# A long convolution: blocked sine-table transforms replaced by one two-stage transform of 4096 points with on-chip shuffles

## The chip, the cores and the metric

One core of one Trainium2 chip. The metric is device time in microseconds (us) from the first to the last instruction plus a fixed start and end (the profiled span is some 1.8 us shorter). Every time of a kernel below is a median of several executions, and every kernel is compared with the kernel before in executions that alternate on the same chip. An execution is called slow when it is over 1.5% above the fastest of the same kernel; ratios use the fast ones.

## The reference

All tensors are bf16, sequence S = 2048, width D = 448, MLP width F = 1792.

```python
def reference(A_q, A_k, A_v, A_shift_k, A_ssm_k, A_ssm_D, B_x, B_w1, B_b1, B_w2, B_b2):
    # mixer on layernorm(q)
    k_shift = sum over t of k_pad[:, t:t+S] * shift_k[:, 3-t]          # 4 taps
    kv   = k_shift * v                                                 # [S, D]
    y    = irfft(rfft(kv padded to 4096) * rfft(ssm_k padded to 4096))[:S]
    y    = y + kv * ssm_D
    h    = A_q + layernorm(A_q) * y
    # MLP along the sequence
    u    = gelu_tanh(einsum("bsd,sf->bdf", layernorm(h), w1) + b1)     # 448 x 1792
    return h + transpose(einsum("bdf,fs->bds", u, w2) + b2)
```

(Shortened: padding, casts and transposes are left out.) The heavy parts are the convolution of 448 channels over 2048 points and the two MLP products.

## The kernel before

The convolution is done in four blocks of 512 points. Each block is transformed by dense products with sine and cosine tables, block spectra are multiplied and summed through the identity matrix on TensorE, and each output tile is transformed back.

```python
def emit_forward(sig, r_sig, blk, dstA, dstB, ...):          # 4 phases x 4 tiles x 2 tables
    for tab, r_tab, dst, r_d in ((NC_t, ..., dstA, ...), (NSf_t, ..., dstB, ...)):
        for phi in range(NPHI):
            for tp in range(TPB):
                op("pe", ... e.matmul(bank(4 + phi), tab[:, tp, 128 * phi: 128 * phi + 128],
                                      sig[:, TPB * blk + tp, :], start=(tp == 0), stop=(tp == TPB - 1)))
            op("act", ... e.copy(out=dst[:, phi, :], in_=bank(4 + phi)))

def emit_products_b(b):                                       # (cut) for every pair of blocks c, j = b - c:
    ...                                                       # 4 products on VectorE, summed on TensorE:
    op("pe", ... e.matmul(bank(bre), ident,  mset[:, 0, q, :], start=first, stop=False))
    op("pe", ... e.matmul(bank(bre), nident, mset[:, 1, q, :], start=False, stop=last))
    ...

def emit_inverse_T(T):                                        # 8 or 16 matmuls per output tile
    ...
def emit_gelu(q, fc):                                         # six instructions, ScalarE and VectorE by turns
    ...
```

w1 is streamed in 32 pieces of 224 KB through a ring; q (normalised) and h go out to DRAM and come back.

## Time and profile before

| | before |
|---|---|
| time, median of 3 (range) | 297.61 us (297.02 to 297.87) |
| TensorE busy | 229.9 us, 78% of the span, 1154 instructions |
| VectorE, ScalarE busy | 178.4 us, 159.4 us |
| granted TensorE clock, mean of later runs | 0.95 to 0.96 |
| DMA | 39.36 MB |
| matmuls of 448 columns | 1088 |

The prediction below shows the lines and reads them.

### The profile page before, as it was taken

Reading aid. Unit: us, or ns where it says so; the run is one execution under the profiler, and the core shown is the slowest. Engines: PE = TensorE matmul, PEld = TensorE weight load, DVE = VectorE, ACT = ScalarE, POOL = GpSimd, SP = SyncE. Lnnn points to the kernel's source line nnn. Section 1 sums busy time; section 2 is a strip of 40 time slices with the busy share of each in tenths; the row PEclk is TensorE's granted clock in tenths of the full one; section 3 lists DMA queues with packets and bytes.
Section 4 is the critical chain, followed back from the end, with each engine's and each line's share of the span. In section 5 each row is a group of like instructions: output and inputs, shape, how many; then the busy total and the mean of one; then the engine's idle time right before and its main releaser. Section 6 shows DMA issues by size and latency. Waiting matters only on the chain.

```text
span 295.9 us, 3832 instructions
## 1 busy us (share of the span) xinstructions
PE 229.9 (78%) x1154; PEld 112.8 (38%) x1154; DVE 178.4 (60%) x426; ACT 159.4 (54%) x335; POOL 33.1 (11%) x81
## 2 busy tenths in 40 slices
PE   0024169999779999899928969759929999799995
PEld 0023124455325555445503425325514444345552
DVE  8959986685998974987187772442244124454131
ACT  2389266998753585867682683854656135610000
POOL 6001120000000032221223031321100000000000
PEclk9999999999979999999975989979987999999999
DMA  6721776658043333221220199436984420025322
GB/s 183 193 74 71 224 232 190 199 173 265 7 149 94 111 113 91 78 78 32 65 62 1 47 320 363 113 109 194 328 329 127 141 107 2 0 62 147 105 62 78
DMA packets 28552, 39.36 MB, mean 133 GB/s; under 512 B 3060, under 2 KB 23670, under 8 KB 28532
## 3 DMA queue, kind: packets, MB, share of 16 engines
q1 hardware_dynamic: 22100, 24.44, 27.5%
q10 hardware_dynamic: 6432, 14.68, 14.7%
q8 instruction: 9, 0.15, 0.2%
q14 instruction: 11, 0.09, 0.1%
HBM read 33.61 MB, written 5.51 MB: 132 GB/s over the span
## 4 chain that ended last, share of the span: by engine, by line
PE 44%; DVE 10%; DMA 8%; ACT 5%; issue 2%; POOL 1%; DVEq 1%; SPq 0%; ACTq 0%
PE ps_all L1046 13%; PE ps_all L1063 12%; PE ps_all L945 8%; PE ps_all L834 4%; DMA XB<-in_B_w_dram 4%; DMA qs<-out_dram 3%; PE ps_all L908 2%; PE ps_all L914 2%; PE ps_all L917 2%; PE ps_all L911 2%; DVE XB L888 1%; DVE XB L890 1%; DMA xs<-in_A_q_dram 1%; DVE XB L886 1%; DVE t1s L962 1%
## 5 line engine op out<-in xcount | busy, mean ns | idle before, releaser
L1046 PE MATMUL ps_all<-hn,XB 128*128 128x448 bf16 x224 | 50.3, 379 | 14.1 <-DMA XB<-in_B_w_dram 6.3
L1063 PE MATMUL ps_all<-XB,YB 128*128 128x448 bf16 x224 | 43.6, 353 | 2.5 <-DVE XB L1036 2.5
L1046 PEld LDWEIGHTS ps_all<-hn,XB 128*128 128x128 bf16 x224 | 22.5, 104 | 40.7 <-issue 13.9
L945 PE MATMUL ps_all<-XB,NC_t 128*128 128x448 bf16 x112 | 32.1, 364 | 1.8 <-ACT XB L924 1.1
L945 PE MATMUL ps_all<-XB,NSi_t 128*128 128x448 bf16 x112 | 32.3, 363 | 0.0
L752 PE MATMUL ps_all<-ident,XB 128*128 128x128 bf16 (+1 forms) x64 | 7.0, 293 | 31.7 <-DMA XB<-in_A_ssm_k_dram 17.3
L1063 PEld LDWEIGHTS ps_all<-XB,YB 128*128 128x128 bf16 x224 | 21.4, 98 | 24.3 <-DVE XB L1036 4.6
L834 PE MATMUL ps_all<-kv,NC_t 128*128 128x448 bf16 x64 | 19.9, 366 | 6.9 <-DVE t1s L962 6.9
L1066 DVE SCALAR_TENSOR_TENSOR osb<-ps_all,b2col,hs 128x448 bf16<-128x448 f32 x16 | 10.5, 681 | 21.6 <-PE ps_all L1063 21.6
L924 ACT CAST XB<-ps_all 128x448 bf16<-128x448 f32 x32 | 16.9, 530 | 10.8 <-PE ps_all L911 8.0
L834 PE MATMUL ps_all<-XB,NC_t 128*128 128x448 bf16 x64 | 21.3, 398 | 0.7 <-ACT XB L761 0.7
L840 ACT ACTIVATE YB<-ps_all,sc 128x448 bf16<-128x448 f32 x32 | 18.7, 632 | 4.8 <-PE ps_all L834 4.7
L844 ACT CAST YB<-ps_all 128x448 bf16<-128x448 f32 x32 | 16.6, 534 | 8.4 <-PE ps_all L834 8.3
L834 PE MATMUL ps_all<-kv,NSf_t 128*128 128x448 bf16 x64 | 19.9, 366 | 0.7 <-ACT YB L844 0.7
L790 DVE TENSOR_TENSOR XB<-XB,Wt 128x1792 bf16<-128x1792 bf16 x16 | 17.1, 1079 | 4.9 <-DMA XB<-in_A_k_dram 4.8
L834 PE MATMUL ps_all<-XB,NSf_t 128*128 128x448 bf16 x64 | 19.9, 352 | 0.0
L1029 DVE SCALAR_TENSOR_TENSOR XB<-XB 128x448 bf16<-128x448 bf16 x14 | 8.8, 625 | 15.9 <-ACT XB L1023 8.4
L752 PEld LDWEIGHTS ps_all<-ident,XB 128*128 128x128 bf16 (+1 forms) x64 | 5.7, 139 | 32.8 <-DMA XB<-in_A_ssm_k_dram 18.4
L821 ACT ACTIVATE qs<-xs,nm_x,rs_x 128x448 bf16<-128x448 bf16 x16 | 12.1, 760 | 9.3 <-DVE nm_x L818 9.0
L908 PE MATMUL ps_all<-XB,ident 128*128 128x448 bf16 x40 | 14.5, 364 | 3.1 <-DVE XB L896 2.8
L945 PEld LDWEIGHTS ps_all<-XB,NC_t 128*128 128x128 bf16 x112 | 11.2, 100 | 13.9 <-ACT XB L924 1.5
L970 ACT ACTIVATE junk<-hs 128x448 bf16<-128x448 bf16 x16 | 9.2, 575 | 12.5 <-DVE hs L966 5.6
(103 smaller groups left out, 386.3 us busy)
## 6 DMA issues: line engine op xcount, KB each, us to landing
XB<-in_B_w_dram ACTq DMA_DIRECT2D x32, 224.0 KB, 2.9
YB<-in_B_w_dram ACTq DMA_DIRECT2D x2, 3584.0 KB, 13.6
XB<-in_A_k_dram SPq DMA_DIRECT2D x15, 448.0 KB, 4.0
xs<-in_A_q_dram SPq DMA_DIRECT2D x32, 112.0 KB, 2.2
XB<-in_A_v_dram SPq DMA_DIRECT2D x16, 112.0 KB, 3.2
out_dram<-qs SPq DMA_DIRECT2D x16, 112.0 KB, 1.7
qs<-out_dram SPq DMA_DIRECT2D x16, 112.0 KB, 2.4
out_dram<-hs SPq DMA_DIRECT2D x16, 112.0 KB, 1.9
```

What stands on the lines that cost most here:

```text
L752: op("pe", lambda e, dst=dst, slot=slot, tt=tt, w=w: e.transpose(out=dst, in_=knat[0:w, slot, 128 * tt: 128 * tt + 128], identity=ident[0: ...
L790: op(E, lambda e: e.tensor_tensor(out=prod, in0=ktap[:, slot, :, :], in1=Wt, op=ALU.mult), reads=[r_ktap[slot], r_Wt], writes=[r_prod[ei]] ...
L821: op("act", lambda e: e.activation(out=qs[:, slot, :], in_=xs[:, slot, :], func=ACT.Identity, bias=nm_x[:, t:t + 1], scale=rs_x[:, t:t + 1 ...
L834: op("pe", lambda e, bk=bk, lhsT=lhsT, tile=tile, tp=tp: e.matmul(bank(bk), lhsT, sig[:, tile, :], start=(tp == 0), stop=(tp == TPB - 1)), ...
L840: op("act", lambda e, bk=bk, dst_ap=dst_ap, scl=scl: e.activation(out=dst_ap, in_=bank(bk), func=ACT.Copy, scale=scl), reads=[Rbank[bk], r ...
L844: op("act", lambda e, bk=bk, dst_ap=dst_ap: e.copy(out=dst_ap, in_=bank(bk)), reads=[Rbank[bk]], writes=[r_d], n=D)
L908: op("pe", lambda e, bre=bre, mset=mset, q=q, first=first: e.matmul(bank(bre), ident, mset[:, 0, q, :], start=first, stop=False), reads=[r ...
L924: op("act", lambda e, bk=bk, dst=dst: e.copy(out=dst, in_=bank(bk)), reads=[Rbank[bk]], writes=[r_Pst[pslot]], n=D)
L945: op("pe", lambda e, lhsT=lhsT, rhs=rhs, ti=ti: e.matmul(bank(bk), lhsT, rhs, start=(ti == 0), stop=(ti == n - 1)), reads=[r_l, r_r], writ ...
L1046: op("pe", lambda e, q=q, slot=slot, t=t: e.matmul(bank(q), w1s[:, slot, 128 * q: 128 * q + 128], hn[:, t, :], start=(t == 0), stop=(t == ...
L1063: op("pe", lambda e, fc=fc: e.matmul(bank(bk), w2sb[:, fc, 128 * T: 128 * T + 128], gT[:, fc, :], start=(fc == 0), stop=(fc == NFC - 1)), ...
L1066: op("dve", lambda e: e.scalar_tensor_tensor(out=osb[:, ob, :], in0=bank(bk), scalar=b2col[:, T:T + 1], in1=hs2[:, fs, :], op0=ALU.add, op ...
```

## The change

Intent: fewer matmuls. With 4096 = 16 x 256 the transform becomes two cheap stages with a shuffle between them: row p of a 16-row group goes from partition to free dimension. The shuffle is a DMA copy from SBUF to SBUF. Everything stays on chip, w1 and w2 are fetched whole, gelu is one ScalarE instruction, and a new list scheduler orders all engines and hands out PSUM banks and staging buffers as it goes. (PSUM is the memory into which TensorE writes its results; the kernel deals it out as eight banks. An eviction is the copy of a result from PSUM to SBUF, by ScalarE or VectorE.) The diff, cut to its core:

```diff
-def emit_forward(...)   # dense 512-point blocks: 256 matmuls
-def emit_products_b(b)  # sums over block pairs through the identity: 160 matmuls
-def emit_inverse_T(T)   # 224 matmuls
+def emit_stage1(src, o_src, T, o_T, tag):
+    for r in range(R):                                   # R = 16
+        b = _Buf(psum, 2)                                # two PSUM banks, given out by the scheduler
+        w = _Buf(wring)                                  # one of 8 staging buffers
+        op("pe", ... e.matmul(Pb(b, 0), Ct[:, r, :], src[:, r, :], start=True, stop=True))
+        op("pe", ... e.matmul(Pb(b, 1), St[:, r, :], src[:, r, :], start=True, stop=True))
+        op(FX, fn, ...)                                  # eviction of 896 elements, ScalarE or VectorE
+        op("sp", ... e.dma_start(T[r:128:R] ..., WR(w.slots[0]) ...), ..., keng=8)   # the shuffle, 229 KB
+def emit_stage2(T, o_T, scale):                          # 16 x 4 matmuls, 16 evictions
+def emit_products_i1():
+    for j in range(R):                                   # 2 products on VectorE, 8 matmuls, 1 eviction
+        ...
+        op("sp", ... e.dma_start(TZ[j:128:R] ..., TU[:, j] ...), ..., keng=8)        # inverse shuffle
+def emit_i2():
+    for g in range(8):
+        for i in range(2):
+            r = 2 * g + i
+            b = _Buf(psum)
+            op("pe", ... e.matmul(Pb(b), ID,  V[:, r, :],         start=True,  stop=False))  # kv * D
+            op("pe", ... e.matmul(Pb(b), CTt[:, r, :], TZ[:, r, 0, :], start=False, stop=False))
+            op("pe", ... e.matmul(Pb(b), STt[:, r, :], TZ[:, r, 1, :], start=False, stop=True))
+            ...                                          # times q, plus x, layernorm
-def emit_gelu(q, fc):    # Identity, Square, 2 x VectorE, Sigmoid, multiply
+def emit_gelu(b, fc):    # one activation
+    op("act", ... e.activation(out=G[:, fc, :], in_=Pb(b), func=ACT.Gelu_apprx_tanh, bias=b1c[:, fc:fc + 1]))
+def emit_w1_load(which) / emit_w2_load():                # whole weights, on ScalarE's DMA queue
+        Pb(b), W2[:, fc, r:S:R], G[:, fc, :], ...        # second product: weight columns 16 apart
+psum = _Pool(8); wring = _Pool(8)
+def can_acquire(o):                                      # an operation may start when its banks are free
+    ...
```

The order in which things are emitted: K's stages, U's first stage (K is the transform of ssm_k, U that of kv), the products with the first inverse step, the second inverse step (`emit_i2`), the MLP.

## The prediction

Passages of the prediction and of the expectations that no trace or run of this case shows are cut, and the places are marked. The sum of the prediction came to 274 us with shuffles of 2.1 us and to 243 with shuffles of 1.43, weighed to 262. Two of its terms are the 2.1 us, and the 0.91 us of an eviction of 896 elements on ScalarE, of which 15 are the 14 us of U's second stage. Both were my assumptions at that point; the trace after shows 2.1 us (229 KB at 108 GB/s from 40 to 60 us) and 0.905 us (L621).

> **What bounds the kernel now.** I read the span in stages first (busy time of each engine in five stretches), because its limits differ by stage, then the chain that ended last, then the groups of instructions for durations.
>
> ```profile
> core 0: us, PE busy (x) PEld busy (x) DVE busy (x) ACT busy (x) POOL busy (x), PEclk, DMA share, GB/s
> 0.00:44.00 44.00, 10.65 (x76) 7.28 (x77) 38.18 (x78) 24.30 (x46) 8.49 (x23) 1.00 0.55 162
> 44.00:196.00 152.00, 131.77 (x646) 63.22 (x643) 106.42 (x278) 103.07 (x233) 22.20 (x53) 0.94 0.40 127
> 196.00:247.00 51.00, 44.52 (x213) 21.16 (x214) 16.17 (x42) 23.85 (x45) 2.36 (x6) 0.90 0.57 187
> 247.00:262.00 15.00, 12.51 (x63) 5.53 (x62) 7.11 (x16) 8.13 (x14) 0.00 (x0) 1.00 0.00 0
> 262.00:296.00 34.00, 30.49 (x162) 15.56 (x159) 10.48 (x16) 0.00 (x0) 0.00 (x0) 0.98 0.33 99
> ```
>
> Up to 44 us VectorE makes sine tables and TensorE idles. From 44 to 196 us the blocked convolution runs: TensorE is busy 131.8 of 152 us with 646 matmuls, so this stage is bound by the count of matmuls. From 196 us on it is the MLP: 100 us for 448 matmuls. The chain shows the dense pace and the holes:
>
> ```profile
> 204.33 10.96 PE ps_all L1046 x58
> 215.29 6.37 DMA XB<-in_B_w_dram
> 221.71 12.12 PE ps_all L1046 x52
> 233.83 4.52 DMA XB<-in_B_w_dram
> ...
> 248.48 0.63 ACT XB L1026
> 249.12 0.47 ACT XB L1034
> 249.61 0.40 DVE XB L1036
> ...
> 261.67 30.83 PE ps_all L1063 x162
> ```
>
> A dense 448-column matmul costs 10.96/58 = 0.189 us, or 30.83/162 = 0.190; in the stretch with the lower clock 12.12/52 = 0.233. Two waits for w1 (6.4 and 4.5 us) and the six-step gelu (14 us between 247 and 262, matmuls in it counted) are MLP overhead. Unit costs for the sum:
>
> ```profile
> L844 ACT CAST YB<-ps_all 128x448 bf16<-128x448 f32 x32 | 16.6, 534 | 8.4 <-PE ps_all L834 8.3
> L790 DVE TENSOR_TENSOR XB<-XB,Wt 128x1792 bf16<-128x1792 bf16 x16 | 17.1, 1079 | 4.9 <-DMA XB<-in_A_k_dram 4.8
> L888 DVE TENSOR_TENSOR XB<-YB 128x896 bf16<-128x896 bf16 x20 | 12.3, 623 | 0.5
> L962 DVE TENSOR_TENSOR t1s<-kv,ps_all 128x448 bf16<-128x448 bf16 x16 | 9.8, 616 | 2.3 <-PE ps_all L945 2.3
> L966 DVE TENSOR_TENSOR hs<-t2s,xs 128x448 bf16<-128x448 bf16 x16 | 6.2, 390 | 2.8 <-DMA xs<-in_A_q_dram 1.4 <-DVE t2s L964 0.5 <-ACT hn L987 0.4
> L970 ACT ACTIVATE junk<-hs 128x448 bf16<-128x448 bf16 x16 | 9.2, 575 | 12.5 <-DVE hs L966 5.6 <-PE ps_all L1046 2.2 <-DVE mv_h L978 2.1
> L970 ACT ACTIVATION_READ_ACCUMULATOR junk<-hs 128x1 f32 x16 | 3.0, 186 | 0.0
> q1 hardware_dynamic: 22100, 24.44, 27.5%
> ```
>
> [...] The second MLP product now reads weights 32 bytes apart; all weights before were packed (about 100 ns), so this is unverified.
>
> **The change part by part.**
>
> *TensorE.* Before: 128+128 matmuls forward, 160 product sums, 224 inverse, 448 MLP = 1088 of 448 columns. After: two signals x (32 + 64) = 192, products with the first inverse step 128, second inverse step 48, MLP 448 = 816, plus 96 transposes. Removed: 272 x 0.19 = 52 us. If TensorE stayed the bound, this alone would give 297 - 52 = 245.
>
> *DMA.* Removed: k read four times (16 x 448 KB becomes 1.8 + 0.3 MB), and q and h through DRAM. Added: 48 shuffles of 128 x 1792 B = 229 KB, 11.0 MB. Sum 8.3 (inputs) + 14.7 (weights) + 1.8 (out) + 11.0 = 36 MB against 39.4: no saving, and the shuffles are now on the path, since each second stage needs all 16 shuffles of the first. Cost of one: queue 1 moved 24.44 MB in 27.5% of 16 x 295.9 us, 18.8 GB/s per engine (queue 10: 21), so eight engines at 20 take 1.43 us[...]. I use 2.1 as the likelier, 1.43 as the rival.
>
> *Path.* Estimates from these costs and from the built order.
> - Loads ahead of the shuffles on SP's queue: 8.3 MB at some 310 GB/s (between the early 209 GB/s at a 0.75 share, 279, and 339 on queue 10): done at 29 us. K's transposes and evictions (4 of 1792 elements) are ready at about 21 us, so the shuffles wait behind the load of x.
> - kv: tables end on VectorE near 11.5 us, then 24 x 1.08 + 16 x 0.62 = 36 us: ready at 47.5. [...]
> - Shuffles of K and U: eight staging slots; evictions from the ninth on wait for a shuffle's semaphore in the built order. 32 x 2.1 = 67 us from 29 on, plus about 6 for w1's first half, issued late in this stretch onto the same engines, plus landing: U complete at about 102 us. TensorE is mostly idle here. VectorE's three evictions of late U slots stand in order ahead of its layernorm work and stall it until 81 us.
> - Second stage of U (64 matmuls, 15 evictions on ScalarE, 14 us), 32 products x 0.623 = 20 us. In VectorE's order a block of layernorm and kv*D work (about 13 us: 9 statistics of 0.6, 5 x 0.62, small ones) stands between the fourth and fifth product. Last product near 137 us.
> - Inverse shuffles: start at 120, ten x 2.1, +4 for w1's second half, landing: 146. ScalarE's queue then holds a w2 load that waits for those ten, ahead of the evictions of the last five; these five then share the engines with 4.2 MB of weights, about 3 us each: everything landed at 165.
> - Second inverse step: VectorE does 15 x (0.616 + 0.39) = 15 us before its first normalisation, so the MLP starts near 165 + 18.5 = 184; ScalarE's statistics, 32 x 0.76 = 24 us, last until 192 and are covered by the first 96+ matmuls.
> - MLP: 448 x 0.194 = 87 us. All w1 and w2 are in time; gelu is one 0.6 us instruction and its matmuls are interleaved, so the holes (11 us of DMA, about 14 of gelu) go. Last addition and store 3 us. Sum: 184 + 87 + 3 = 274.
>
> With 1.43 us per shuffle, U is complete near 82, the last inverse shuffle at 134, the MLP starts at 153: 243.
>
> **The rivals.** *Shuffles are engine-limited or spread over 16 engines*: 243 or less; for it, queue rates of about 20 GB/s per engine and a program that allows for eight engines[...]. *TensorE remains the bound*: 245, by the arithmetic above; against it, the three points where a whole stage must land before the next can start. *Strided weights slow the second MLP product*: if a load rose from 0.1 to 0.4 us, 224 x (0.4 - 0.19) = 47 us would be added, 290 to 320. For it, nothing before has such weights; against it, [...]loads overlap matmuls (PEld busy 15.6 of 34 us at the end)[...]. *Weights beside the last inverse shuffles*: without this contention the first sum would be about 262.
>
> **Range and chances.** I weigh 274 at 0.6 and 243 at 0.4: 262 us. The range 238 to 285 covers both with some error in the load rate (3 us) and clock (0.85 instead of 1 in half of the MLP: +8). 285 leaves out most of the strided-weight case, to which I give 8%. Below 291.7 is faster by over 2%: 0.89; within 2%: 0.06; slower: 0.05.
>
> **What would show each step.** TensorE about 170 us busy for 912 instructions; a hole in its activity before U's second stage (near 75 to 100 us) and another before the second inverse step; in both, the chain naming the on-chip copy (arena from arena). Time from issue to landing of the shuffles of 2 us when alone and far more when queued; 16 in a row spaced 2.1 us[...] or 1.4 us (engines). DMA share near 0.5 in this stretch if only eight engines work. MLP matmuls at 0.19 us and weight loads of the last product still about 0.1 us. No gelu hole. The prediction is wrong below 238 if shuffles are cheaper than 1.4 us or run on 16 engines, and above 285 if weight loads or landing times are longer than assumed.

## More of the kernel before

TensorE has 44% of the span on the chain of work that ended last, DMA 8%. One line adds to this, the clock granted to TensorE in 40 slices of the span, in tenths (9 is 90% or more):

```profile
PEclk9999999999979999999975989979987999999999
```

TensorE, busy for 78% of the span, was granted 0.95 of its full clock over it.

## The result, and the profile after

The changed kernel is correct and slower: **321.1 us** (317.69 to 326.04, 5 executions) against 297.61 (296.29 to 298.53, 5 executions of the same session). The ratio of the fast runs is 1.0749, 95% interval 1.0682 to 1.0816. A ratio is the mean time of one kernel's fast runs over that of the other's of the same rounds, so it is not quite the ratio of the medians. The recorded trace is one of two executions of 326 us that count as slow (granted clock 0.783 against 0.80 in the fast ones), so its stage times are up to some 2% long; the effects below are far larger.

| | predicted | measured after |
|---|---|---|
| one shuffle | 2.1 us (rival 1.43) | 2.1 us |
| U complete (last shuffle of U landed) | 102 | 104.8 |
| first inverse shuffle issued | 120 | 150.9 |
| last inverse shuffle landed | 165 | 213.7 |
| MLP on the chain from | 184 | 229.3 |
| MLP to the end | 90 | 95 |
| TensorE busy | about 170 us | 213.5 us (x913) |
| time | 262 (274 with 2.1 us shuffles) | 321.1 |

The page of the changed kernel, two rows of the slices and the chain that ended last by engine and line (DMA as a whole has 31% of it, 8% before):

```profile
PEclk9978555559795665555599959559599999999999
DMA  7996555555996000001229579629500000000022
...
DMA arena<-arena 28%; PE ps L1034 13%; ACT arena L621 10%; PE ps L888 10%; PE ps L854 8%; PE ps L1025 8%; PE ps L1017 6%; DMA arena<-in_A_ssm_k_dram 3%; ACT arena L839 3%; DVE arena L958 2%; DVE arena L961 1%; PE ps L817 1%; DVE arena L1037 1%; SPq L743 0%; DVE arena L624 0%
```

"arena<-arena" is the shuffle: 28% of the span. The DMA row has six slices at 5, further on five at 0, and then rises again: two shuffle phases with a gap between them in which no data moves. The clock row shows 5 or 6 in the gap.

Two stretches, busy time of each engine, granted clock, DMA share and rate:

```profile
core 0: us, PE busy (x) PEld busy (x) DVE busy (x) ACT busy (x) POOL busy (x), PEclk, DMA share, GB/s
40.00:60.00 20.00, 8.29 (x19) 1.19 (x18) 7.04 (x9) 8.15 (x9) 0.00 (x0) 0.50 0.54 108
120.00:140.00 20.00, 12.98 (x32) 3.50 (x32) 7.65 (x24) 6.33 (x7) 4.40 (x7) 0.50 0.00 0
```

From 40 to 60 us the shuffles of K and U run alone: 108 GB/s, at a share of 0.54, near the 0.5 that was foreseen for eight engines of sixteen (no view here shows the engines singly). 229 KB at 108 to 110 GB/s is 2.1 us each, the likelier figure of the prediction. From 120 to 140 us nothing moves by DMA and no engine is near full: TensorE 65%, at half its clock, ScalarE 32%, VectorE 38%. This is the stretch to explain. The chain there:

```profile
119.09 0.91 ACT arena L621
...
120.05 1.69 PE ps L854 x4
121.76 0.91 ACT arena L621
...
150.94 3.18 PE ps L888 x8
154.15 0.91 ACT arena L621
...
179.52 8.83 DMA arena<-arena
188.37 0.37 ACTq L1004
...
201.93 11.76 DMA arena<-arena
```

L854 is the second stage, L888 the products with the first inverse step, L621 the eviction. Four matmuls, then the eviction, then four matmuls: 119.09 to 121.76 is 2.67 us for a row, and from 110 us on the two do not overlap on this chain. Further down, ScalarE waits 8.8 us for shuffles at L1004, the issue of a load of w2, and at the end there are 11.8 us of shuffles alone. Why TensorE should wait for an eviction when there are eight PSUM banks is in the order of TensorE's instructions as built (position of the group, line, operation, shape, count; the groups of the trace have the same order):

```
66 L854 Matmult ps<-arena 128x448 x52
67 L864 Matmult ps<-arena 128x128 x16
68 L951 Matmult ps<-arena 128x448 x4
69 L864 Matmult ps<-arena 128x128 x13
70 L854 Matmult ps<-arena 128x448 x4
71 L864 Matmult ps<-arena 128x128 x3
72 L854 Matmult ps<-arena 128x448 x4
73 L951 Matmult ps<-arena 128x448 x2
74 L854 Matmult ps<-arena 128x448 x56
75 L888 Matmult ps<-arena 128x448 x128
```

L951 is the identity matmul that opens the accumulation of kv*D in the second inverse step. It depends on nothing but kv*D, so the scheduler fills idle TensorE time with six of them. Each opens a bank that is only closed after the last inverse shuffle has landed, at 213.7 us. Six banks of eight are gone; the 56 + 128 matmuls that follow have one pair of banks to take turns in. I had read this order before I predicted, and had not asked what rows 68 and 73 hold.

**Theory.** (A) The held banks take the overlap of matmul and eviction away and with it half of TensorE's clock. (B) The weights: one load of w2 stands in ScalarE's queue and waits for shuffles, ahead of evictions, and the weights share the DMA engines with the inverse shuffles. (C) The shuffle itself, if the partitions that it writes make the 2.1 us, is a cost that another layout could halve. **Rivals.** The low clock is there by itself; the shuffles would be as slow without weights; the engines, of which the kernel counts on eight, and not the partitions make the 2.1 us; the gelu part costs something here.

### The profile page after: what moved, and what is told of

Its sections match the earlier page's. It is cut to its first block, busy times and chain, and to the rows that moved or that the text cites. A ratio compares the mean times of both kernels' runs of the same rounds, so it can differ in the third digit from the quotient of the medians.

```text
span 324.2 us, 2484 instructions
## 1 busy us (share of the span) xinstructions
PE 213.5 (66%) x913; PEld 96.8 (30%) x913; DVE 121.5 (37%) x241; ACT 110.0 (34%) x168; POOL 18.3 (6%) x45
## 4 chain that ended last, share of the span: by engine, by line
PE 47%; DMA 31%; ACT 13%; DVE 5%; issue 1%; SPq 1%; DVEq 0%; ACTq 0%
DMA arena<-arena 28%; PE ps L1034 13%; ACT arena L621 10%; PE ps L888 10%; PE ps L854 8%; PE ps L1025 8%; PE ps L1017 6%; DMA arena<-in_A_ssm_k_dram 3%; ACT arena L839 3%; DVE arena L958 2%; DVE arena L961 1%; PE ps L817 1%; DVE arena L1037 1%; SPq L743 0%; DVE arena L624 0%
## 5 line engine op out<-in xcount | busy, mean ns | idle before, releaser
L854 PE MATMUL ps<-arena 128*128 128x448 bf16 x128 | 43.0, 491 | 31.1 <-ACT arena L621 13.6
L621 ACT CAST arena<-ps 128x896 bf16<-128x896 f32 (+1 forms) x32 | 28.2, 881 | 78.7 <-PE ps L854 38.0
L888 PE MATMUL ps<-arena 128*128 128x448 bf16 x128 | 34.4, 424 | 20.8 <-ACT arena L621 20.8
L1034 PE MATMUL ps<-arena 128*128 128x448 bf16 x224 | 45.6, 355 | 0.0
L1037 DVE SCALAR_TENSOR_TENSOR arena<-ps,arena 128x448 bf16<-128x448 f32 x16 | 9.7, 677 | 69.0 <-PE ps L1034 69.0
L839 ACT CAST arena<-ps 128x896 bf16<-128x896 f32 x29 | 25.6, 931 | 29.4 <-DMA arena<-arena 26.2
L1034 PEld LDWEIGHTS ps<-arena 128*128 128x128 bf16 x224 | 31.5, 145 | 13.5 <-ACT arena L1008 3.1
L832 PE MATMUL ps<-arena 128*128 128x448 bf16 x32 | 16.0, 501 | 25.7 <-ACT arena L839 19.9
L854 PEld LDWEIGHTS ps<-arena 128*128 128x128 f16 x128 | 13.2, 119 | 59.8 <-ACT arena L621 23.8
L1025 PE MATMUL ps<-arena 128*128 128x448 bf16 x128 | 29.4, 353 | 0.0
L1017 PE MATMUL ps<-arena 128*128 128x448 bf16 x96 | 23.7, 386 | 5.8 <-DVE arena L983 5.8
L877 DVE TENSOR_TENSOR arena<-arena 128x896 bf16<-128x896 bf16 x16 | 10.0, 625 | 43.5 <-PE ps L888 42.6
L888 PEld LDWEIGHTS ps<-arena 128*128 128x128 f16 x128 | 12.9, 111 | 42.6 <-ACT arena L621 29.9
L1008 ACT ACTIVATE arena<-ps,arena 128x448 bf16<-128x448 f32 x14 | 8.9, 633 | 40.4 <-PE ps L1017 21.1
L958 DVE TENSOR_TENSOR arena<-ps,arena 128x448 bf16<-128x448 f32 x16 | 9.4, 623 | 29.7 <-PE ps L955 29.6
L798 DVE TENSOR_TENSOR arena<-arena 128x1792 bf16<-128x1792 bf16 x16 | 16.5, 1098 | 4.0 <-DMA arena<-in_A_k_dram 4.0
L832 PEld LDWEIGHTS ps<-arena 128*128 128x128 f16 x32 | 3.3, 102 | 46.7 <-ACT arena L839 38.5
L834 PE MATMUL ps<-arena 128*128 128x448 bf16 x32 | 16.5, 516 | 0.0
L1025 PEld LDWEIGHTS ps<-arena 128*128 128x128 bf16 x128 | 12.0, 98 | 12.6 <-ACT arena L1008 2.4
L964 ACT ACTIVATE arena<-arena 128x448 bf16<-128x448 bf16 x16 | 9.2, 576 | 17.3 <-PE ps L953 16.9
L1017 PEld LDWEIGHTS ps<-arena 128*128 128x128 bf16 x96 | 10.1, 106 | 16.3 <-DVE arena L983 6.3
L953 PE MATMUL ps<-arena 128*128 128x448 bf16 x16 | 6.8, 425 | 11.2 <-DMA arena<-arena 11.2
```

What stands on the lines that cost most here:

```text
L621: return e.copy(out=dst(), in_=src())
L798: op("dve", lambda e, W, T=T, i=i, r=r: e.tensor_tensor(out=T[:, i], in0=KH[:, r:r + 4, :], in1=WT, op=ALU.mult), r=[(o_KH + r * DB, 4 * D ...
L832: op("pe", lambda e, W, b=b, r=r: e.matmul(Pb(b, 0), Ct[:, r, :], src[:, r, :], start=True, stop=True), r=[r_C(r), (o_src + r * DB, DB)], ...
L834: op("pe", lambda e, W, b=b, r=r: e.matmul(Pb(b, 1), St[:, r, :], src[:, r, :], start=True, stop=True), r=[r_S(r), (o_src + r * DB, DB)], ...
L839: return e.copy(out=dst, in_=Ppair(b)) if W == "act" else e.tensor_copy(out=dst, in_=Ppair(b))
L854: op("pe", lambda e, W, b=b, bi=bi, tab=tab, ci=ci, st=st, sp=sp, j=j: e.matmul(Pb(b, bi), tab, T[:, j, ci, :], start=st, stop=sp), r=rr, ...
```

## The experiments

Twelve kernels ran, all correct. Times in the table are medians of all executions, slow ones included; stage times come from each trace (us from the start). The kernels ran in four sessions on different chips, where the kernel before had medians of 296.8 to 297.5 us, so differences between kernels of different sessions carry some 1 us of doubt.

| kernel | U complete | inverse shuffles: first issued, last landed | MLP from | time (range) | ratio of fast runs to before, 95% |
|---|---|---|---|---|---|
| after | 104.8 | 150.9, 213.7 | 229.3 | 321.1 (317.7 to 326.0) | 1.0749, 1.0682 to 1.0816 |
| e1_no_prefill | 104.2 | 126.2, 184.3 | 199.9 | 297.6 (295.4 to 299.0) | 1.0022, 0.9947 to 1.0097 |
| e2_prefill4 | 102.1 | 126.1, 182.5 | 198.1 | 294.8 (291.8 to 295.5) | 0.9893, 0.9820 to 0.9965 |
| e10_w2late | 104.5 | 127.4, 179.7 | 195.2 | 289.9 (289.0 to 292.3) | 0.9767, 0.9710 to 0.9824 |
| e5_wlate | 93.5 | 122.3, 160.7 | 181.0 | 277.8 (277.0 to 279.3) | 0.9367, 0.9311 to 0.9422 |
| e12_wlate_sp | 96.2 | 124.6, 163.0 | 178.6 | 273.8 (271.9 to 274.4) | 0.9192, 0.9125 to 0.9259 |
| e4_perm | 84.9 | 106.9, 164.7 | 180.3 | 275.9 (275.6 to 296.0) | 0.9273, 0.9215 to 0.9332 |
| e7_permj | 84.6 | 106.9, 155.2 | 170.8 | 276.4 (267.9 to 285.8) | 0.9054, 0.8981 to 0.9127 |
| e6_wlate_perm | 75.2 | 103.2, 140.3 | 160.9 | 262.3 (256.8 to 275.4) | too few fast runs |
| e8_ports8 | 75.0 | 97.4, 156.9 | 172.4 | 268.8 (267.4 to 269.3) | 0.9051, 0.9001 to 0.9100 |
| e11_ports8_wlate | 65.1 | 91.0, 127.9 | 143.5 | 238.2 (236.9 to 240.1) | 0.8009, 0.7946 to 0.8072 |
| e9_ports8_wlate_j | no fast trace | no fast trace | | 235.5 (234.4 to 463.0) | 0.7913, 0.7866 to 0.7959 |
| e3_before_gelu1 | | | | 292.6 (291.2 to 293.4) | 0.9833, 0.9775 to 0.9892 |

### 1 and 2: the held banks

e1 forbids any identity matmul to start before the products are done. e2 allows four of the sixteen early, so four banks are held and two pairs stay.

```diff
 op("pe", ... e.matmul(Pb(b), ID, V[:, r, :], start=True, stop=False), r=[...], bw=[b], n=D,
+   after=i1_last if r >= 0 else ())          # e1; in e2: r >= 4
```

In e1 the scheduler also gives out pairs of neighbouring banks only; e2 has no such rule.

> The identity matmuls of kv*D may no longer run ahead: they wait for the last inverse-step matmul, so they hold no PSUM banks during U's second stage and the products (pairs of banks are also kept adjacent, as they always were in the changed kernel). Theory A, six of eight PSUM banks were held by early identity matmuls and left one pair, so TensorE and ScalarE took turns: a row of U's second stage falls from 2.68 us to about 1.0, a row of products from 2.65 to 4.1 us to about 1.5; the stretch from U landed (104.9) to the last inverse shuffle landed (213.7) falls from 109 us to 60 to 70 us (sixteen shuffles of 2.09 us plus the weights beside them then bound it); time 272 to 285. Theory B, the low clock of TensorE is the cause and not its consequence: rows stay at 1.7 and 3.2 us, time about 300. Theory C, ScalarE's evictions and VectorE's order bound the stretch anyway: under 10 us gained, above 310.

> The same with four identity matmuls allowed ahead: four banks held, two pairs left. Theory A: two pairs are enough to let TensorE work beside an eviction, so nearly all of the gain of the first run: 275 to 290, rows of U's second stage at 1.0 to 1.3 us. If the loss grew in proportion with the banks held, the gain would be a third of it: about 305.

Measured: 297.6 and 294.8 us. From U complete to the first inverse shuffle it is 22 and 24 us instead of 46. The chain of e1 in this stretch:

```profile
104.20 4.76 PE ps L860 x17
...
108.98 0.91 ACT arena L627
...
109.94 2.65 PE ps L860 x13
```

Seventeen and thirteen second-stage matmuls follow one another without an eviction on the path. The busy times of e1 and of e2 from 120 to 140 us, where the changed kernel had 12.98 (x32) and a clock of 0.50:

```profile
120.00:140.00 20.00, 15.42 (x76) 7.21 (x74) 19.95 (x50) 7.10 (x9) 5.16 (x8) 0.94 0.38 75
```

```profile
120.00:140.00 20.00, 16.41 (x82) 7.52 (x83) 14.05 (x33) 9.49 (x12) 3.04 (x5) 1.00 0.43 80
```

More than twice the matmuls in the same time, at a clock of 0.94 and 1.00. By then e1 and e2 are at a later part of the work; like for like, U's 64 second-stage matmuls took 555 ns each in the mean after and 380 in e1, and from 105 to 143 us the clock was 0.54 after, 0.93 in e1 and 0.92 in e2. A row of U's second stage fell from 2.67 us to 15.5/16 = 0.97 in e1, the 1.0 that was expected. So theory A holds: in this stretch the low clock is a consequence, since only the order of the instructions and the banks they get were changed. e2 settles two side questions: a second pair of banks is enough (no more is gained by the other two), and the neighbour rule is not what helped. The size was overestimated: I had expected 272 to 285 (e2: 275 to 290) and got 297.6 (294.8). The stretch from U complete to the last landing fell from 109 us to 80 in e1 where 60 to 70 was expected, since the wait for the shuffles took over a part of what was gained. In e1 the first inverse shuffle is issued at 126.2 and the last lands at 184.3, 58 us for 16 shuffles of 2.1 us. That is theory B's part:

```profile
145.71 14.18 DMA arena<-arena
...
159.91 0.37 ACTq L1010
...
163.18 21.13 DMA arena<-arena
```

ScalarE's queue comes to L1010, the issue of w2, at 145.7 and stands there for 14.2 us until shuffles have landed; its next eviction, and with it the next shuffle, comes after that. Then the last shuffles take 21.1 us beside the weights.

### 3, 4, 5: the weights

```diff
# e10: w2 only, from SyncE, after the first second-inverse matmul (the inverse shuffles have landed)
-op(WQ, ... dma_start(W2 ...), ...)
+op("sp", ... dma_start(W2 ...), ..., after=[first["i2"]])
# e5: w1's first part from SyncE once U's second stage runs; w1's second part and w2
#     from ScalarE's queue once the inverse shuffles have landed
-op(WQ, ... dma_start(W1A ...), ...)
+op("sp", ... dma_start(W1A ...), ..., after=[first[o_TU]])
+... W1B, W2: after=[first["i2"]]
# e12: as e5, but W1B and W2 issued from SyncE
```

All three are built on e1.

> e1 with only the load of w2 moved: issued from SyncE after the inverse shuffles have landed; both parts of w1 stay where the change has them, on ScalarE's queue. Theory Q (the 14.2 us in which ScalarE stands at the w2 load that waits for ten shuffles is what costs): that wait is gone, inverse shuffles landed at 168 to 174 instead of 184.4, time 280 to 288. Theory B (it is the DMA engines shared with the weights): landed at 180 or later, time 292 or more. e5, which moved all weights, stands at 277.8; what is left between this run and e5 is the share of w1.

> e1 with the weights moved: the first part of w1 is issued from SyncE after the first product matmul of U has started, its second part and w2 from ScalarE's queue only after the inverse shuffles have landed. Theory W (in e1 the weights cost twice: 14.2 us in which ScalarE stood at a w2 load that waited for ten shuffles, and some 14 us in which the last shuffles shared the DMA engines with the weights): U landed near 97 to 102, inverse shuffles landed about 155 to 162 instead of 184.4, time 268 to 278. Rival S (shuffles are limited by their own 2.09 us whatever runs beside): landed near 175 to 180, time 288 to 295. Rival L (weights late for the MLP, which then waits): landed early, but the MLP takes over 100 us instead of 92.

> e5 with the weights that follow the inverse shuffles issued from SyncE, since in e5 they held ScalarE up between the shuffles and the MLP (20.2 us from the last landing to the first MLP matmul, 15.5 in the changed kernel). This kernel has what the prediction took for granted: no bank held by an early identity matmul, and no weight transfer in the way of shuffles or evictions; its shuffles are as the change has them, 2.09 us each. If the sum of the prediction holds once these two hold: U landed 93 to 98, inverse shuffles landed 158 to 163, the MLP starts 15 to 18 us later, time 264 to 271 (the prediction said 262). If a further cost is still unfound: 274 or more.

Measured: e10 289.9, e5 277.8, e12 273.8 us. In e10 the 14 us in front of L1010 are gone, yet the last shuffle lands only 4.6 us earlier than in e1: the end of its shuffle phase is still slow, beside w1's second part, whose two loads are issued at 140.0 and 151.3 us (137.1 and 148.4 in e1):

```profile
159.94 19.74 DMA arena<-arena
```

So theory Q, which put the cost on the blocked queue, was too narrow (its 168 to 174 us and its 280 to 288 both missed), and B too (its "292 or more" missed by 2 us): moving w2 is worth 7.7 us of time, and moving w1's two parts 16.0 us more (e10 to e12, where all moved loads come from SyncE; 12.1 to e5, which issues the late ones from ScalarE). The 7.7 us are not the queue alone, since e10 also takes w2's traffic off the last shuffles; no run separated the two. e5 is within theory W's ranges (landed 160.7, 277.8 us; U complete even earlier than its 97 to 102), and its MLP takes 94 us, so the weights do not come late. e5 and e12 have all weights out of the way, and the shuffles end thus in e12:

```profile
153.66 9.37 DMA arena<-arena
```

Where e10 has 19.7 us on its chain for the last shuffles, e12 has 9.4. From the first issue to the last landing it is 38.4 us, of which 16 x 2.1 = 33.6 are the shuffles' own. U is also complete 8 to 11 us earlier than in e1, as w1's first part no longer shares the engines with U's last shuffles. In e5 the late weights stood in ScalarE's way in front of the MLP (20.2 us from the last landing); e12 mends that (15.6). e12 came out at 273.8 where 264 to 271 was expected.

### 6, 7, 8, 9: the shuffle's 2.1 us

Two ways to test whether the partitions that a shuffle writes make it; that they do is theory P in what follows. e4 (on e1) keeps each shuffle as it is and changes only the order, so that neighbours in time land four partitions apart instead of one: r = 0, 4, 8, 12, 1, 5, ... e7 does the same for the inverse shuffles. e8 (on e1) keeps the order and changes where one shuffle lands: partitions (r & 3) + 32 (r >> 2) + 4q instead of r + 16q, with three small tables permuted to match.

```diff
# e4
-for r in range(R):
+for r in [4 * (x % 4) + x // 4 for x in range(R)]:
# e8
-e.dma_start(T[r:128:R] ..., WR(w.slots[0]) ...)
+e.dma_start(T[(r & 3) + 32 * (r >> 2):(r & 3) + 32 * (r >> 2) + 29:4] ..., WR(w.slots[0]) ...)
```

> The first run with the first stage's sixteen r in the order 0, 4, 8, 12, 1, 5, ...[...]. If [...]the eight engines move in step, the spacing stays 2.09 us (229 KB at 110 GB/s) and the time is that of the first run within 1%. If engines can drift apart over two shuffles in flight, the spacing falls towards 1.43 us (20 GB/s per engine), U lands near 85 us and the time falls by up to 20 us.

> e4 with the j order of the inverse shuffles permuted as well, weights where the change has them. Theory P[...]: inverse shuffles landed some 6 to 12 us before e4's 164.8, time 262 to 270. Theory W (here the weights and the queue of ScalarE set the end): within 3 us of e4's 275.9.

> e1 with the 16 partitions of stage 1 laid out[...]; the order of the shuffles is the original. Theory P[...]: K and U shuffles at most 1.43 us each, 160 GB/s or more at the same share of eight engines, U landed at 80 to 88 instead of 104.2, time 272 to 284. Rival E (eight engines make it): still 108 to 111 GB/s, U landed within 3 us of 104, time 294 to 300.

> e5 with both shuffles also issued in an order [...](r in steps of four, as in e4, and j likewise). If both gains add (e4 gained 21.7 us on e1, e5 some 22): U landed near 77 to 85, inverse shuffles landed near 130 to 140, time 238 to 255. If they are the same gain twice, time 268 to 276.

Measured: e4 275.9, e8 268.8. The stretch from 40 to 60 us, where the changed kernel had 108 GB/s, first in e4, then in e8:

```profile
40.00:60.00 20.00, 13.85 (x33) 3.11 (x33) 7.11 (x9) 13.32 (x16) 0.00 (x0) 0.50 0.53 168
```

```profile
40.00:60.00 20.00, 16.00 (x54) 4.34 (x53) 11.71 (x17) 14.11 (x16) 0.21 (x1) 0.72 0.55 203
```

168 and 203 GB/s, where e1 had 108 at the same busy share of the DMA engines (0.53 and 0.55 against 0.54). In e8 the first load of w1 falls into the last 2.4 us of this stretch; e11, where no weights do, has 201 GB/s at a share of 0.52. So the engines were occupied just as long with less data. 229 KB at 201 GB/s is 1.14 us a shuffle, and below even the prediction's rival of 1.43. U is complete at 75.0 instead of 104.2, earlier than the 80 to 88 that theory P expected, and the time of 268.8 is below its 272 to 284. This is a direct test, as e8 changes neither bytes nor order and the busy share of the engines stays the same: the partitions that a shuffle writes set its rate here, 108 GB/s in e1 and 201 in e11. Why these partitions are faster no trace shows. For e4 the second of its two expectations came true (U complete at 84.9, 21.7 us gained). Whether engines drift apart in e4, as that expectation had it, is not shown: no trace here follows single engines. What is shown is that the order alone took the rate from 108 to 168 GB/s.

The j order (e7 against e4) brings the last inverse shuffle 9.5 us forward and the fast executions to 268 to 270 us, within the 262 to 270 of theory P. But e4, e6 and e7 have slow executions (one of four, two of four, two of four), with a lower clock in the same kernel (e4 0.813 against 0.842 to 0.853, e6 0.853 and 0.867 against 0.875 and 0.881, e7 0.828 and 0.84 against 0.856 and 0.871); e1, e2, e5, e8, e10, e11 and e12 have none. Nothing here shows why the permuted order does this.

e6 adds late weights and both orders: 256.8 and 258.9 us in its two fast executions, above the 238 to 255 expected. Here too the late weights were in ScalarE's queue: issuing them held it for some 9 us between the shuffles and the MLP (6.7 and 2.6; the 2.6 are on the chain), and the MLP starts 20.6 us after the last landing, where e12 has 15.6.

### 10 and 11: all together

> e9 without the j order[...]. If inverse shuffles are produced slower than 2.09 us apart the order costs nothing, and this is within 3 us of e9[...].

> All that helped, together: the partition layout of e8, the late weights of e5, the j order of e7; and the weights that are fetched after the inverse shuffles are issued from SyncE, since in e6 they stopped ScalarE for some 9 us. If the gains add: U landed at 68 to 75 us, inverse shuffles landed at 118 to 130, the MLP starts 15 to 18 us after that and takes 88 to 92, time 225 to 242. If the weights come too late for the MLP, time 245 to 256.

e11 (layout of e8, late weights from SyncE) takes 238.2 us, all four executions between 236.9 and 240.1; e9 adds the j order: 234.4, 234.7 and 236.3 us, and 463.0 us in a fourth. The recorded trace is unluckily that fourth. In it every group of 96 or more 448-column matmuls, in all stages, has a mean of 755 to 759 ns, twice the 353 to 386 of the MLP's groups in the changed kernel, while the last addition on VectorE takes as long as there (0.68 us, on the chain, and 0.677). So TensorE was slow and VectorE, as far as this instruction shows, was not. The record gives a granted clock of 1.00, but the page of this execution has no clock row at all; what slowed it stays open.

The fast times of e9 are within the 225 to 242 that were expected. Whether the j order acts as e11's expectation has it can't be told without a fast trace of e9; in time, e11 is 3.5 us behind e9's fast median. Against e12, from which it differs only by the layout, e11 gains 35.6 us. Of the two I would keep e11, 20% faster than the kernel before and 1% behind e9. The MLP starts at 143.5 us, and the 94 us after it are now the largest stage.

### 12: gelu alone

e3 is the kernel before with gelu as one instruction and nothing else.

> The kernel before with one part of the change alone: the gelu as one ScalarE instruction from PSUM in place of three ScalarE and three VectorE instructions. As I counted in the prediction (about 14 us of gelu hole): ratio 0.955, 284 us. Rival: in the 15 us from 247 to 262 TensorE did run 63 matmuls, 12 us at 0.19, so the true hole is 3 us: ratio 0.985 to 0.99, 293 to 295 us.

It gains 5 us (ratio 0.9833; it is faster, but whether by 2% is unclear), not the 14 us of the hole and a little more than the rival had. In e3 the wait for w1 on the chain is now one of 11.0 us, as long as the two of before together (6.4 and 4.5), and the hole itself had 62 matmuls of the second product in it, so it was less of a hole than I took it for:

```profile
247.00:262.00 15.00, 12.51 (x62) 5.53 (x62) 1.00 0.00 0
```

These are the second product's matmuls in the kernel before, 12.5 us busy in the 15 us of the "hole".

## Why the prediction was wrong

**The step that failed** is "Second stage of U (64 matmuls, 15 evictions on ScalarE, 14 us), 32 products x 0.623 = 20 us", together with "Inverse shuffles: start at 120": it took evictions for the limit, with matmuls running beside them. With one pair of banks left, a row cost matmuls plus eviction, 2.67 us instead of 0.91, with the clock at half. The first inverse shuffle was issued 46.1 us after U was complete, where 18 had been worked out. e1 gives 22.0, so the held banks are 24 us of the 28 us that this term was short. In time of the whole kernel, taking them away is worth some 22 us between the fast executions (319.4 on average, and 297.4 in e1). The other 4 us are there in every kernel without held banks that has just U's 64 second-stage matmuls left when U lands (22.0 to 22.9 us in e1, e4, e7, e8 and e10): 18.1 of the 22.0 us are matmuls on the chain of e1 and 2.7 evictions, so even without held banks it is mostly the matmuls that take the time there and not the evictions.

**A second term was too small**: the weights beside the inverse shuffles. The prediction had both mechanisms (w2 ahead of the evictions in ScalarE's queue, and shared engines) and 12 us for them in the last inverse shuffles. From first issue to last landing it had 45 us; it was 62.8 after, 58.1 in e1, and 38.4 in e12 without weights. So weights cost some 20 us there, and another 8 us ahead of U's last landing (6 had been allowed). Moving them away is worth 23.8 us in all (e1 to e12).

Together: U complete to last landing was 108.9 us, predicted 63; the excess of 46 is 28 before the first inverse shuffle and 18 after it. Of these 18, the held banks made 4.7 (62.8 to 58.1 in e1), the weights 7.7 beyond the 12 allowed, and 5.4 are still there in e12 (38.4 against 33).

**What held.** Shuffles of 2.1 us at a DMA share of 0.54, so the case of 2.1 us was the right one of the two that were mixed, at 274 us, and the number 262 was the weighing of it with a wrong one. U complete at 102 (104.8 measured). The two holes with "arena from arena" on the chain. Strided weights are not slow enough to matter: the load takes longer than in the packed product, but lies beside the matmuls:

```profile
L1034 PEld LDWEIGHTS ps<-arena 128*128 128x128 bf16 x224 | 31.5, 145 | 13.5 <-ACT arena L1008 3.1
...
L1025 PEld LDWEIGHTS ps<-arena 128*128 128x128 bf16 x128 | 12.0, 98 | 12.6 <-ACT arena L1008 2.4
```

145 ns a load (strided) against 98 (packed), where the prediction's sign was "still about 0.1"; but 13.46 us for 70 of its matmuls is 0.192 each. The rival that had given them 47 us is refuted. MLP at 0.19 us a matmul, 95 us from its start in the slow trace against 90. Two smaller readings did not hold: TensorE was busy for 213.5 us and not 170, as its matmuls ran at a mean clock of 0.78 (an estimate from that: 170/0.78 = 218), and VectorE makes sine tables only up to 27 us of the kernel before, not 44; from there to 44 us it works on kv.

**Is the sum right once its assumptions hold?** e12 has free banks and no weights in the way, and takes 273.8 us. That it equals the 274 of the prediction is a coincidence: without contention the same working says 262, and 256 with U earlier by the 6 us that were given to w1. Against that, e12 has U complete at 96.2 (96), the stage from there to the last landing 66.9 (51, that is 153 - 102), the MLP 15.6 later (18.5), 94 us of MLP (90) and some 1 us around the span. So the stage is 16 us longer than worked out even then: 10 us of it before the first inverse shuffle (28.5 against 18), and the rest in the shuffles themselves, 38.4 against about 33. Of the 10 us, 4 are those of e1 above. The other 6 I put down to K: of the second-stage line 91 matmuls run between 96 and 130 us, and only 64 of them are U's, so 27 are left over from K; the first 20 of that line take 6.0 us at a low clock (0.67 from 80 to 100 us). The other traces agree: with 64 left it is 22.0 to 22.9 us (five kernels), with 80 left 25.9 (e11), with 91 left 28.0 to 28.8 (e5, e6, e12). In the changed kernel and in e1 nothing of K was left when U landed (64 of the 128 matmuls of this line run before, 64 after), so this is a cost of the late weights' order and no part of the prediction's miss.

**The range** of 238 to 285 and 5% for slower did not contain a case in which the order of the scheduler costs anything. All rivals were about how fast known work goes; none asked what the order holds back.

What stays open: the slow executions of the permuted orders, the 463 us execution, and the 5 us by which e12's inverse shuffles take longer than worked out.

## What to carry to other kernels

When a scheduler may run an operation early, ask what that operation takes and until when it keeps it: here six opening matmuls of an accumulation, 0.35 to 0.58 us each, kept six of the eight PSUM banks until the last inverse shuffle had landed (213.7 us), which cost some 22 us. One pair of banks was too few for a stage that evicts (321.1 us), two were enough (e2, 294.8). A chain that shows an engine and its eviction taking strict turns (1.69 and 0.91 us), with the clock at half (0.50) and no engine full, was the sign of too few banks here; the order of instructions on that engine then tells which earlier one took them. For on-chip shuffles, try which partitions the target lies on (2.1 us a shuffle before, 1.14 with the layout of e8, as e11 has it), keep bulk loads out of the stretch in which they run (23.8 us here, e1 to e12), and do not put a load that waits into the queue of an engine that has evictions to do (ScalarE's stood for 14.2 us in e1).
